# A long convolution beside a gated MLP: filter, convolution and most of the MLP in 64x64 TensorE tiles in place of 128x128 and 32x32

## The chip, the cores and the metric

One core of one Trainium2 chip. The metric is the device time of one execution in microseconds (us), the median of several runs; lower is better.

## What is computed

Two branches read the same layer-normed input. Branch A is a causal long convolution over 2048 positions in 512 channels, branch B a gated MLP with 1792 inner features.

```
xn = layernorm(A_q)                                   # 2048 x 512
kv = (sum over t of k shifted by t * shift_k[t]) * v   # four taps
y  = irfft(rfft(kv, 4096) * rfft(ssm_k, 4096))[:2048] + kv * ssm_D
s  = xn * y
h  = gelu(xn @ w_gate) * (xn @ w_up)                   # 512 -> 1792
out = A_q + s * silu(h @ w_down)                       # 1792 -> 512
```

All inputs and the output are bf16.

## The kernel before

**The convolution** is a transform of 4096 points in two stages. Stage 1 multiplies 128 partitions by a 128x256 matrix `F1` with full 128x128 matmuls (two per row tile, 512 columns each): for the filter from its transposed halves `HTr` and `HTD` (`half1`, `stage1_h`), for the key product from `V` (`stage1_k`). The results are evacuated, stored to the scratch tensors ZH and ZK in HBM and read back with other rows on the partitions, as `BH` and `BK`. Stage 2 is 32 small transforms of 32 points, each with its own twiddled matrix in `TF`; `tiles` (L1023 ff.) runs sixteen 32x32 matmuls side by side, one for each tile of the array, 512 columns each: `fwd` for BH and BK in eight groups. The filter's spectrum lands in `HS`, a copy with swapped partners is made by DMA (`HW`), VectorE multiplies both by the key's spectrum `KB`, and the inverse stage 2 (`inv` in `spectrum`) adds two rounds of sixteen tiles, with `MI`. `BO` is stored to ZI, read back as `BI`, and the output transform `y` (L1201) multiplies with `G1`, four full matmuls for two row tiles.

**The filter** comes with channels on the partitions. Half of it is transposed by TensorE (`h_transpose`, L878, pairs of bf16 read as one fp32 word), half by DMA (`HTD`).

**The MLP.** The 2048 rows are cut into four quarters of 512 (q = 0 to 3). `unit(q, m)` computes 128 inner features: four matmuls into a gate bank and four into an up bank of PSUM, a gelu on ScalarE (L1137), a product on VectorE (L1140). For q = 0 the first two units work in halves of 256 rows. `down(q)` computes each of four row tiles from fourteen matmuls (L1156); for q < 3 a tanh and a VectorE op make the gate from it, for q = 3 a silu, and the last row tile is cut into 384 and 128 columns.

**What sets the order.** All of this is a list of tasks. The string `SEQ` names them in the order in which they are issued, on all engines; a small model (`Sched.run`) only hands out buffer slots along the way. Each engine runs its own part strictly in this order, waiting on semaphores where data or a buffer is not ready; loads and stores are issued mostly from SP, some from ScalarE's queue. PSUM has eight banks, in four pairs. Nearly every TensorE, copy and DMA instruction is issued from one line (L618, L609, L612, L590), so the profile names them by their tiles: `psall<-xnT,Wu` is an up matmul, `psall<-Wd,HT` a down matmul, `psall<-V,F` stage 1 of the key, `psall<-BH,TF` and `psall<-BK,TF` forward stage 2 (L1028), `psall<-HS,MI` and `psall<-HW,MI` its inverse, `psall<-BI,G` the output transform, `psall<-ident,Hn` the filter's transposes.

Of the kernel before, what the change touches and what calls it, by code (L numbers as in the profile page):

```python
# [14 lines left out]
DM = 512  # L15
# [37 lines left out]
LOAD_NS = {("x0_", 262144): 1400.0, ("x0_", 131072): 450.0, 262144: 900.0, 524288: 1350.0, ("x", 524288): 2100.0, ("h", 524288): 1300.0, ("wg", 524288): 1550.0, ("wu", 524288): 1450.0, 917504: 2620.0, ("sk", 524288): 1500.0, 344064: 1250.0, 46080: 350.0, 3072: 100.0, 1024: 200.0}  # L53
# [5 lines left out]
N_HALF = 2  # L59

# [214 lines left out]
class Buf:  # L275


    def __init__(self, name, pool=None):
# [4 lines left out]
        self.readers = []  # L283
        self.left = 0
        self.last_end = 0.0


class Task:
    __slots__ = ("n", "opts", "r", "w", "emit", "deps", "lat", "nbytes", "start", "end", "eng", "outs", "heavy", "mode")


class Sched:


    SEM = 90.0
# [3 lines left out]
    DMA_BW = 370.0  # L299
    SHARE_BW = 300.0  # L300
    FIRST = {"loads": 1050.0, "SP": 30500.0}
    DRAIN = 121.0
    EARLY, TAKEN, SHARED, WAIT = (0.0, 1.0), 1400.0, 46000.0, 3300.0
    LANDS = (4350.0, 5590.0, 7100.0, 8420.0, 9350.0, 10200.0, 11500.0)

# [981 lines left out]
```

## Time and profile before

| | before |
|---|---|
| median of the timed runs (lowest, highest) | 194.69 us (194.65, 195.05) |
| span of the profiled execution | 193.3 us |
| TensorE matmuls, busy | 1377, 188.6 us |
| VectorE, ScalarE, GpSimd busy | 160.0, 125.4, 13.9 us |
| moved by DMA | 49.19 MB |

The profiled execution has no time of its own beside its span: the timed runs include 1.4 us more, around the span. "Busy" counts a matmul from its start to its modelled end, and these overlap. A row of a timeline gives the start, the length from the first start to the last end, the engine and line, out<-in, and how many instructions it merges; brackets hold idle time before it and who ended it. A row of a group ends with its count, busy time, the mean length of one in ns, and the idle time before its instructions.

### The profile page before, as it was taken

How to read it: one execution, taken by the hardware profiler on the slowest of the kernel's cores; microseconds unless marked ns; L12 is line 12 of the kernel's file. 1: busy time of each engine (PE TensorE's matmuls, PEld its weight loads, DVE VectorE, ACT ScalarE, POOL GpSimd, SP SyncE). 2: the span in 40 equal slices, each digit the busy share in tenths (PEclk: the TensorE clock that was granted, in tenths of full speed). 3: DMA queues.
4: the chain of work that ended last, by engine and by line, in shares of the span. 5: the costliest groups of instructions: out<-in, count | busy, mean ns of one | idle time of the engine just before them, and what ended most of it. 6: DMA issues, size and time to landing. Idle time of an engine off the chain costs nothing.

```text
span 193.3 us, 3502 instructions
## 1 busy us (share of the span) xinstructions
PE 188.6 (98%) x1377; PEld 85.6 (44%) x1377; DVE 160.0 (83%) x245; ACT 125.4 (65%) x170; POOL 13.9 (7%) x32
## 2 busy tenths in 40 slices
PE   7899999999999999999999999999999999999993
PEld 2685544444444444443434433433444334444452
DVE  6699789998999995877888789878897863588993
ACT  6787999969885987868548766856577431232121
POOL 5412420000000000020300000000000000000000
PEclk9999999999999999999999999999999999999999
DMA  5999999999999679999999991984805345939333
GB/s 175 311 307 349 377 400 347 157 249 372 375 374 354 196 264 259 390 323 305 218 285 230 338 320 59 288 276 147 264 10 195 106 140 153 389 112 353 132 139 136
DMA packets 45958, 49.19 MB, mean 254 GB/s; under 512 B 12787, under 2 KB 39671, under 8 KB 45942
## 3 DMA queue, kind: packets, MB, share of 16 engines
q1 hardware_dynamic: 37366, 42.67, 70.1%
q10 hardware_dynamic: 8576, 6.29, 10.3%
q8 instruction: 11, 0.18, 0.4%
q14 instruction: 5, 0.04, 0.1%
HBM read 27.39 MB, written 14.68 MB: 218 GB/s over the span
## 4 chain that ended last, share of the span: by engine, by line
PE 93%; DMA 4%; SPq 1%; DVE 1%; ACT 0%; issue 0%
PE psall L618 86%; PE psall L1028 5%; DMA Hn<-in_A_ssm_k_dram 4%; PE psall L854 1%; SPq L590 1%; PE psall L878 1%; DVE G L1175 0%; DVE G L1174 0%; ACT G L1172 0%
## 5 line engine op out<-in xcount | busy, mean ns | idle before, releaser
L618 PE MATMUL psall<-xnT,Wu 128*128 128x512 bf16 (+1 forms) x232 | 55.8, 372 | 0.0
L618 PE MATMUL psall<-xnT,Wg 128*128 128x512 bf16 (+1 forms) x232 | 55.3, 372 | 0.0
L618 PE MATMUL psall<-Wd,HT 128*128 128x512 bf16 (+2 forms) x238 | 52.0, 367 | 0.0
L1140 DVE TENSOR_TENSOR HT<-psall,GE 128x512 bf16<-128x512 f32 x54 | 36.7, 685 | 15.8 <-PE psall L618 15.4
L1137 ACT ACTIVATE GE<-psall 128x512 bf16<-128x512 f32 x54 | 31.7, 601 | 13.1 <-PE psall L618 12.9
L618 PEld LDWEIGHTS psall<-Wd,HT 128*128 128x128 bf16 x238 | 22.4, 98 | 25.9 <-issue 1.1
L618 PEld LDWEIGHTS psall<-xnT,Wg 128*128 128x128 bf16 x232 | 21.9, 98 | 25.4 <-issue 1.3
L618 PEld LDWEIGHTS psall<-xnT,Wu 128*128 128x128 bf16 x232 | 21.6, 98 | 25.9 <-issue 3.5
L609 ACT ACTIVATE X<-psall 128x1024 bf16<-128x1024 f32 (+1 forms) x18 | 15.1, 843 | 3.3 <-DMA ZH<-X 1.9
L609 ACT ACTIVATE HS<-psall 128x1024 bf16<-128x1024 f32 x14 | 13.7, 1022 | 4.4 <-PE psall L1028 4.4
L1164 ACT ACTIVATE G<-psall 128x512 bf16<-128x512 f32 x12 | 7.0, 598 | 12.9 <-PE psall L618 12.4
L1011 DVE TENSOR_TENSOR KAC<-KAC,KTM 128x2048 bf16<-128x2048 bf16 x12 | 14.6, 1217 | 0.1
L1009 DVE TENSOR_TENSOR KTM<-KK,SKB 128x2048 bf16<-128x2048 bf16 x12 | 14.6, 1217 | 0.0
L609 ACT ACTIVATE BO<-psall 128x1024 bf16<-128x1024 f32 x9 | 9.1, 1022 | 8.2 <-PE psall L1028 7.7
L609 ACT ACTIVATE KB<-psall 128x1024 bf16<-128x1024 f32 x11 | 11.0, 1021 | 3.6 <-PE psall L1028 3.6
L609 ACT ACTIVATE AST<-psall 128x1024 bf16<-128x1024 f32 x12 | 12.4, 1033 | 0.7 <-PE psall L618 0.5
L612 DVE CAST BO<-psall 128x1024 bf16<-128x1024 f32 x7 | 8.5, 1224 | 3.7 <-PE psall L1028 3.7
L821 DVE BATCH_NORM_STATS2 stats<-X 128x6 f32<-128x512 bf16 x16 | 10.3, 675 | 1.1 <-DMA X<-in_A_q_dram 1.1
L1172 ACT ACTIVATE G<-psall 128x512 bf16<-128x512 f32 (+2 forms) x5 | 2.6, 512 | 13.1 <-PE psall L618 13.1
L1091 DVE TENSOR_TENSOR HW<-KB,HW 128x1024 bf16<-128x1024 bf16 x16 | 10.9, 682 | 0.0
L1091 DVE TENSOR_TENSOR HS<-KB,HS 128x1024 bf16<-128x1024 bf16 x16 | 10.8, 682 | 0.0
L1166 DVE SCALAR_TENSOR_TENSOR G<-G,psall 128x512 bf16<-128x512 bf16 x12 | 7.8, 680 | 2.0 <-ACT G L1164 2.0
(83 smaller groups left out, 175.6 us busy)
## 6 DMA issues: line engine op xcount, KB each, us to landing
BH<-ZH SPq DMA_DIRECT2D x8, 512.0 KB, 6.1
HW<-HS SPq DMA_DIRECT2D x16, 256.0 KB, 3.2
BK<-ZK SPq DMA_DIRECT2D x8, 512.0 KB, 5.1
ZI<-BO ACTq DMA_DIRECT2D x16, 256.0 KB, 2.8
BI<-ZI SPq DMA_DIRECT2D x8, 512.0 KB, 4.2
ZK<-AST SPq DMA_DIRECT2D x6, 512.0 KB, 4.1
Hn<-in_A_ssm_k_dram SPq DMA_DIRECT2D x4, 512.0 KB, 8.4
KK<-in_A_k_dram SPq DMA_DIRECT2D x4, 512.0 KB, 8.6
```

The lines of the kernel that those rows point to most:

```text
L609: return h.activation(o, i, ACTF.Copy, scale=scale)
L612: return h.tensor_copy(o, i)
L618: return h.matmul(o, lhsT=l, rhs=r, start=st, stop=sp)
L821: t_stats[t] = op([("DVE", 670.0)], lambda e, h, t=t: h.bn_stats(stats[:, t, :], X[:, t, :]), r=[bX[q][t % 4]], w=[bst[t]], rr=[R_X[t]], w ...
L1009: op([("DVE", dur)], lambda e, h, j=j, m=m: h.tensor_tensor(KTM[:, m.slot, :, :], kk(j), sk(j), ALU.mult), r=need + [bSKB[j], a], w=[m], r ...
L1011: op([("DVE", dur)], lambda e, h, m=m: h.tensor_tensor(KAC[:, a.slot, :, :], KAC[:, a.slot, :, :], KTM[:, m.slot, :, :], ALU.add), r=[m], ...
L1028: trk.op("PE", lambda h: h.matmul(ps(s, i)[b, :], lhsT=wt(col)[a, :], rhs=data(col)[a, :], start=n < 16, stop=n >= len(todo) - 16, tile_po ...
L1091: return hd.tensor_tensor(o, flat(KB, kb[h]), o, ALU.mult)
L1137: op([("ACT", act(512))], lambda e, h: h.activation(GE[:, g.slot, :], bank(pg), ACTF.Gelu_apprx_tanh), r=[pg], w=[g], rr=lambda: R_bank(pg ...
L1140: op([("DVE", dve(512, 1))], lambda e, h: h.tensor_tensor(HT[:, q % 2, m, :], bank(pu), GE[:, g.slot, :], ALU.mult), r=[pu, g], w=[bHT[q][m]],
L1164: op([("ACT", act(n))], lambda e, h, g=g, pc=pc: h.activation(g, pc(), ACTF.Tanh, scale=0.5), r=[p], w=[bt], rr=lambda p=p: R_bank(p), ww= ...
L1166: op([("DVE", dve(512, 1))], lambda e, h, g=g, pc=pc: h.scalar_tensor_tensor(out=g, in0=g, scalar=1.0, in1=pc(), op0=ALU.add, op1=ALU.mult ...
```

## The change

Between the transposes of the filter and the last two row tiles, every matmul becomes a 64x64 tile of the array, four of them side by side making a round (`quads`). The rows of the sequence are dealt out so that the two halves of the partitions hold the even and the odd blocks of 16 rows (`rows`). The transform of 4096 points is split 64 by 32 on each half: stage 1 needs one round for what took two full matmuls, stage 2 has 64x64 matrices and takes two rounds where one round of sixteen tiles served. Tables (`TF`, `MI`, `TFA`) grow accordingly and are made by GpSimd where VectorE made them.

A 64x64 tile adds up 64 partitions only, and in the kernel the two row halves of the array always write different banks. So a unit and a pair of row tiles of `down` use a pair of banks in two phases: in the first, the lower half of the partitions adds to bank 0 and the upper to bank 1, in the second the other way round. The first matmul of the second phase waits for the end of the first (`own`, and `hand` in the list). The same holds for the output transform.

The filter's transposes are 64x64 bf16 matmuls with the identity. Four pairs of row tiles (`N_RAW`) are copied out raw, and get one silu of 1024 elements after the last gelu in place of a tanh each. `SEQ` is a new order, and the order of the loads changes with it. All ahead of the core is left out here: table making, addresses, names.

```diff
+        def quads(rounds, own=False, cols=None):
+            todo = [(n, *x) for n, x in enumerate(x for rnd in rounds for x in rnd)]
+            for n, pair, i, r, c, wt, data, rt, st, sp in todo:
+                w = R_ps[pair] if own and n == 0 else [R_ps[pair][i]]
+                trk.op("PE", lambda h: h.matmul(ps(pair, i)[HALF[c], cols(n) if cols else slice(0, 512)], lhsT=wt, rhs=data, start=st, stop=sp, tile_position=(64 * r, 64 * c)),
+                       r=rt, w=w, accum=not (own and n == 0), quiet=n < len(todo) - 1)
...
-                        trk.op("PE", lambda h, o=o, src=src: h.transpose(o, src, ident32[:]), r=[R_Hn[k], R_id32], w=R_bank(pp[hf]), accum=True)
+                quads([[(psl(p), r, r, b, src[HALF[r], 8 * hf + j, b, :], ident[HALF[r], HALF[r]], [R_Hn[k], R_id], True, True) for r in range(2) for b in range(2)] for j in range(8)], cols=lambda n: slice(64 * (n // 4), 64 * (n // 4) + 64))
...
+        def fwd1(pair, data, rd):
+            for b in range(2):
                 for c in range(2):
-                    trk.op("PE", lambda h, c=c: mm(h, bank(p)[:, 256 * c:256 * c + 256], F1[:, c, :], HTr[:, u, 256 * k:256 * k + 256], True, True), r=[R_F1, R_HTr[u][k]], w=R_bank(p), accum=True)
+                    o, n = slice(64 * c, 64 * c + 64), slice(64 * b, 64 * b + 64)
+                    trk.op("PE", lambda h: h.matmul(ps(pair, b)[o, :], lhsT=F1[n, o], rhs=data[n], start=True, stop=True, tile_position=(64 * b, 64 * c)),
+                           r=[R_F1, *rd], w=[R_ps[pair][b]], accum=True, quiet=b + c < 2)
...
-        def fwd(pp, T, R_T, buf, n):
-            return lambda e: tiles(pp, [(lambda c: TF[:, 4 * n + c, :], lambda c: T[:, buf.slot, c, :], [R_MF, R_T[buf.slot]])])
+        def fwd(p, T, R_T, buf, n, h):
+            return lambda e: quads([[(psl(p), r, r, c, TF[HALF[r], 4 * n + 2 * h + c, :], T[HALF[r], buf.slot, 2 * h + c, :], [R_MF[n // 4], R_T[buf.slot]], True, True) for r in range(2) for c in range(2)]])
...
-            def inv(e):
-                tiles(pi, [(lambda c, m=m: MI[:, m, n, 32 * c:32 * c + 32], lambda c, T=T, b=b: T[b.slot][:, c, :], [R_MI[m], *R_b])
             for h in range(2):
+                def inv(e, h=h):
+                    quads([[(psl(pi[h]), r, r, c, MI[HALF[r], m, 2 * n + h, 64 * c:64 * c + 64], T[b.slot][HALF[r], 2 * h + c, :], [R_MI[m], *R_b], m == 0, m == 1) for r in range(2) for c in range(2)]
...
-            tg = S.add([("PE", pe(4))], half(pg, Wg, "g"), r=[bW["g"][ci]] + bxnT[q], w=[pg], lat=200.0)
-            tu = S.add([("PE", pe(4))], half(pu, Wu, "u"), r=[bW["u"][ci]] + bxnT[q], w=[pu], lat=200.0, after=[tg])
+            def phase(ph):
+                def f(e):
+                    quads([[(psl(p), (r + ph) % 2, r, c, (Wg, Wu)[(r + ph) % 2][HALF[r], kd, 128 * m + 64 * c:128 * m + 64 * c + 64], xnT[HALF[r], q % 2, 0:4, kd, :],
+                             [R_Wc["gu"[(r + ph) % 2], ci], *R_xnT[q % 2]], ph == 0 and kd == 0, ph == 1 and kd == KD - 1) for r in range(2) for c in range(2)] for kd in range(KD)], own=ph == 1)
+            hand = None
+            for ph in range(2):
+                hand = S.add([("PE", 4 * T_ROUND)], phase(ph), r=[bW["g"][ci], bW["u"][ci]] + bxnT[q], w=[p], lat=200.0, mode=1, hand=hand)
...
+            for i, (ph, m0, m1) in enumerate(((0, 0, 4), (0, 4, 9), (1, 0, 4), (1, 4, 9), (1, 9, 14), (0, 9, 14))):
+                own = i in (2, 5)
+                hand = S.add([("PE", (m1 - m0) * T_ROUND)], part(ph, m0, m1, i == 0, i == 5, own), r=bHT[q][m0:m1] + bWd[m0 // 7:(m1 + 6) // 7], w=[p], lat=200.0, mode=1, hand=hand if own else None)
...
-                        trk.op("PE", lambda h, i=i, c=c: mm(h, ps(s, i), G1[:, c, :], BI[:, bi.slot, 2 * i + c, :], c == 0, c == 1),
+                    quads([[(psl(p), (r + ph) % 2, r, c, G1[HALF[r], 0:64], BI[HALF[r], bi.slot, 2 * ((r + ph) % 2) + c, :], [R_G1, R_BI[bi.slot]], ph == 0, ph == 1) for r in range(2) for c in range(2)]], own=ph == 1)
...
+            if j < N_RAW:
+                op([("ACT", act(1024, True))], lambda e, h, g=g: h.activation(g, g, ACTF.Silu), r=[bG[j]], w=[bGX[j]], rr=R_G[ts], ww=R_G[ts], after=gelu_tasks)
```

Three places of TensorE's order show what it moves. First the start: the beginning of TensorE's list before, from the second filter block (h1) on.

```order
L878 MATMUL psall<-ident_63,Hn 128x128 x8
L618 MATMUL psall<-xnT,Wg 128x256 x4
L618 MATMUL psall<-HTr,F_58 128x256 x2
L854 MATMUL psall<-ident,XN 128x128 x4
L618 MATMUL psall<-xnT,Wu 128x256 x4
```

And of the change, from the x transposes behind the first filter block (h0), with what each waits for; d_wg1 and d_wu1 are the landings of the second group of weights:

```order
L858 MATMUL psall<-ident,XN 128x128 [waits s_DVE]
L858 MATMUL psall<-ident,XN 128x128 x3
L620 MATMUL psall<-xnT,Wu 128x256 [waits d_wu0,s_DVE]
L620 MATMUL psall<-xnT,Wu 128x256 x3
L620 MATMUL psall<-xnT,Wg 128x256 [waits d_wg0]
L620 MATMUL psall<-xnT,Wg 128x256 x3
...
L933 MATMUL psall<-HTr,F_55 64x512 [waits s_ACT]
L933 MATMUL psall<-HTr,F_55 64x512 x3
L878 MATMUL psall<-xnT,Wg 64x512 [waits d_wg1,s_DVE]
L878 MATMUL psall<-xnT,Wg 64x512
L878 MATMUL psall<-xnT,Wu 64x512 [waits d_wu1,s_ACT]
```

The h1 block has moved behind the first units in 64x64 tiles, and between the first weights and those units only half units and one round of stage 1 are left. Second, the hand-over on TensorE where units and stage 1 of the key mix: behind a unit's first phase comes other work, then its second phase, which waits for TensorE's own semaphore.

```order
L878 MATMUL psall<-xnT,Wu 64x512 x2
L933 MATMUL psall<-V,F_55 64x512 [waits s_ACT]
L933 MATMUL psall<-V,F_55 64x512
L933 MATMUL psall<-V,F_55 64x512 [waits s_DVE]
L933 MATMUL psall<-V,F_55 64x512
L933 MATMUL psall<-HTD,F_55 64x512 [waits s_ACT]
L933 MATMUL psall<-HTD,F_55 64x512 x3
L878 MATMUL psall<-xnT,Wu 64x512 [waits s_PE]
```

Two rounds of stage 1 lie between the phases here. There are 76 such hand-overs; between the phases lie no round in 5 of them, one in 10, two or more in 61. Third, the first inverse transforms, before:

```order
L618 MATMUL psall<-Wd,HT 128x512 x14
L1028 MATMUL psall<-HS_56,MI 32x512 x16
L1028 MATMUL psall<-HW_96,MI 32x512 x16
L618 MATMUL psall<-xnT,Wg 128x512 x8
L618 MATMUL psall<-xnT,Wu 128x512 x4
```

and of the change, among forward transforms of the key and the phases of units:

```order
L878 MATMUL psall<-BK,TF 64x512 x8
L878 MATMUL psall<-Wd,HT 64x512 x20
L878 MATMUL psall<-xnT,Wg 64x512 x2
L878 MATMUL psall<-xnT,Wu 64x512 x2
...
L878 MATMUL psall<-HS_93,MI 64x512 x4
L878 MATMUL psall<-HW_95,MI 64x512 x4
L878 MATMUL psall<-xnT,Wu 64x512 x2
```

All shapes are now the same here; the list has 128x128 matmuls left in the warm-up, the transposes of x with the half units (at two places), and the last two row tiles. In all TensorE has 3205 matmuls in place of 1377.

More of the change, by code (lines that the diff above doesn't have):

```diff
@@ L59 @@
 N_HALF = 2
+N_RAW = 4
 class Res:
@@ L288 @@
 class Task:
-    __slots__ = ("n", "opts", "r", "w", "emit", "deps", "lat", "nbytes", "start", "end", "eng", "outs", "heavy", "mode")
+    __slots__ = ("n", "opts", "r", "w", "emit", "deps", "lat", "nbytes", "start", "end", "eng", "outs", "heavy", "mode", "hold", "hand")
 class Sched:
@@ L317, in add @@
         t.start = t.end = t.eng = None
-        t.mode = mode
+        t.mode, t.hold, t.hand = mode, list(hold), hand
         deps = {}
@@ L333, in add @@
             b.writers.append(t)
-        for b in set(t.r + t.w):
+        for b in set(t.r + t.w + t.hold):
             b.left += 1
@@ L356, in run @@
                 base = max(base, d.end if eng == d.eng == "PE" else d.end + d.lat + (self.SEM if not d.nbytes or eng != "PE" else 400.0 if d.eng == "loads" else self.HEDGE))
-            for b in t.w:
+            if t.hand is not None:
+                base = max(base, t.hand.end + self.HAND)
+            for b in t.w + t.hold:
                 if b.pool is not None and b.slot is None:
@@ L376, in run @@
                 t.end = pipe + self.DMA_LAT / 2 + (self.WAIT if en < self.SHARED else 0.0)
-            for b in set(t.r + t.w):
+            for b in set(t.r + t.w + t.hold):
                 b.left -= 1
@@ L474, in build_kernel @@
         place["at"] = kk_at + 2048
[L475 to L476 removed]
+        HS = [new(f"HS{j}", [128, 4, DM], BF16) for j in range(3)]
+        HW = [new("HW0", [128, 4, DM], BF16), *[at(f"HW{j}", [128, 4, DM], BF16, ast_at + 4096 * (j - 1)) for j in (1, 2)]]
         KB = new("KB", [128, 4, 2, DM], BF16)
@@ L604, in emit @@
                 trk.op(e, lambda h: fn(e, h), r=R, w=W)
-            return S.add(engs, emit, r=r, w=w, lat=lat, after=after)
+            return S.add(engs, emit, r=r, w=w, lat=lat, after=after, hold=hold)
         def copy(e, h, o, i, scale=1.0):
@@ L890, in build_kernel @@
+        for k in range(2):
+            for hf in range(2):
+                h_transpose(k, hf)
         h_perm, h_dtr = [], []
@@ L936, in stage1_h @@
             if x == "H" and u >= 4:
-                for k in range(2):
-                    half1(u, k, a)
+                aH[u] = a
+                if u % 2:
+                    for k in range(2):
+                        half1(u - 1, k)
             else:
@@ L1020, in z_rows @@
             return bass.AP(Z, g * 128 * DM, [[DM, 128], [128 * DM, n], [1, DM]])
-        def tiles(pp, terms):
-            todo = [(wt, data, rt, row, col) for wt, data, rt in terms for row in range(4) for col in range(4)]
-            for n, (wt, data, rt, row, col) in enumerate(todo):
-                a, b = slice(32 * row, 32 * row + 32), slice(32 * col, 32 * col + 32)
-                s, i = psl(pp[row // 2]), row % 2
-                trk.op("PE", lambda h: h.matmul(ps(s, i)[b, :], lhsT=wt(col)[a, :], rhs=data(col)[a, :], start=n < 16, stop=n >= len(todo) - 16, tile_position=(32 * row, 32 * col)),
-                       r=rt, w=[R_ps[s][i]], accum=True, quiet=n < len(todo) - 1)
@@ L1181, in build_kernel @@
+        def down(q):
+            down_pair(q, 0)
+            if q < NQ - 1:
+                down_pair(q, 2)
+                return
+            for jt in (2, 3):
+                down_tile(q, jt)
         for q in range(NQ):
```

386 lines of the change are left out of this document (199 added, 187 removed), and 45 rows, old and new, of the table SEQ.

## The prediction

> **What bounds the kernel now.** I read the page's busy lines first, then the chain of waits in order of time, then who waited for whom on TensorE, then TensorE's groups by shape. The page and the chain:
>
> ```profile
> PE 188.6 (98%) x1377; PEld 85.6 (44%) x1377; DVE 160.0 (83%) x245; ACT 125.4 (65%) x170; POOL 13.9 (7%) x32
> ...
> PEclk9999999999999999999999999999999999999999
> ...
> PE 93%; DMA 4%; SPq 1%; DVE 1%; ACT 0%; issue 0%
> ```
>
> ```profile
> 2.12 7.16 DMA Hn<-in_A_ssm_k_dram
> ...
> 30.27 51.16 PE psall L618 x238
> 81.42 0.36 PE psall L1028 x16
> ...
> 189.55 0.02 issue
> ```
>
> The waits of TensorE behind its first real matmul at 5.64 us are two short ones:
>
> ```profile
> PE psall L878 <- DMA Hn<-in_A_ssm_k_dram: 0.5, 1, 0.5
> PE psall L618 <- ACT HTr L609: 0.2, 1, 0.2
> ```
>
> So from 9.3 to 189.6 us TensorE runs without a gap at full clock, and what its work costs is what the kernel costs: a nanosecond taken out of TensorE's stream is a nanosecond of time, as long as nobody makes it wait instead. The span is 193.3 us; the timed runs have a median of 194.69, so 1.4 us lie around the span, and I carry that over. The stream, by shape (count | busy us, mean ns):
>
> ```profile
> L618 PE MATMUL psall<-xnT,Wu 128*128 128x512 bf16 x216 | 53.6, 380 | 0.0
> ...
> L618 PE MATMUL psall<-Wd,HT 128*128 128x512 bf16 x210 | 49.0, 379 | 0.0
> L618 PE MATMUL psall<-V,F 128*128 128x512 bf16 x32 | 9.2, 379 | 0.0
> L618 PE MATMUL psall<-BI,G 128*128 128x512 bf16 x32 | 7.6, 379 | 0.0
> ...
> L618 PE MATMUL psall<-HTD,F 128*128 128x512 bf16 x16 | 4.6, 379 | 0.0
> L1028 PE MATMUL psall<-BK,TF 32*32 32x512 bf16 x128 | 3.5, 385 | 0.0
> L1028 PE MATMUL psall<-HS,MI 32*32 32x512 bf16 x128 | 3.5, 385 | 0.0
> L1028 PE MATMUL psall<-BH,TF 32*32 32x512 bf16 x128 | 3.5, 385 | 0.0
> L1028 PE MATMUL psall<-HW,MI 32*32 32x512 bf16 x128 | 3.4, 374 | 0.0
> ...
> L618 PE MATMUL psall<-HTr,F 128*128 128x256 bf16 x16 | 2.9, 274 | 0.2 <-ACT HTr L609 0.2
> ...
> L618 PE MATMUL psall<-HTr,F 128*128 128x512 bf16 x8 | 2.4, 379 | 0.0
> ```
>
> The 379 ns is one matmul from start to end; they overlap. The pace, and the price of changing the tile shape, come from the timeline of TensorE around one inverse transform:
>
> ```profile
> 97.45 3.20 PE L618 MATMUL psall<-Wd,HT 128*128 128x512 bf16 x14
> 100.58 0.43 PE L1028 MATMUL psall<-HS,MI 32*32 32x512 bf16 x16
> 100.81 0.42 PE L1028 MATMUL psall<-HW,MI 32*32 32x512 bf16 x16
> 101.16 1.90 PE L618 MATMUL psall<-xnT,Wg 128*128 128x512 bf16 x8
> ```
>
> Fourteen matmuls take 3.20 us, the last of them 0.379: (3.20 - 0.379) / 13 = 0.217, and over longer runs 0.216 us each. A "round" of sixteen 32x32 tiles with 512 columns takes as long as one full matmul: HS to HW is 0.23 us. From 97.45 to 101.16 are 3.71 us for 14 matmuls and 2 rounds, 16 x 0.216 = 3.46: going into 32x32 tiles and out again costs **0.25 us**. The four L1028 rows hold 512 / 16 = 32 rounds in 24 such visits (8 forward H, 8 forward K, 8 inverse with two rounds).
>
> **The change, part by part**, on TensorE's stream. A round is now four 64x64 matmuls with 512 columns, priced at 0.216: the same array, fully covered, as a full matmul. Both tiled and full rows above show that pace, but no row shows a 64x64 round; the bounds are 0.216 below (two forms so different keep it, and neither is faster) and 0.234 above (worked out under the rivals).
>
> 1. Stage 1 and the output transform do half the work each. Before: 32 + 16 + 8 + 32 full matmuls and 16 of half width, (88 + 8) x 0.216 = 20.7 us. Now 32 rounds of stage 1 and 16 of the output, 48 x 0.216 = 10.4. **-10.3 us.**
> 2. Stage 2 does twice the work: 32 rounds become 64 (16 forward H, 16 forward K, 32 inverse). **+6.9 us.**
> 3. The switches go: 24 x 0.25 = 6.0. By the order, the new stream has three stretches of 128x128 left (the transposes of x with half units, twice, and the last two row tiles), so three trips, one of which lies in the idle start. Two on the path, 0.5. **-5.5 us.**
> 4. The units and the down projections keep their work: 432 full matmuls of the units become 432 rounds, 196 of the 210 full ones of the down projections become 196 rounds. 0 us.
> 5. The filter's transposes:
>
> ```profile
> 5.64 1.71 PE L878 MATMUL psall<-ident,Hn 128*128 128x128 f32 x8
> 7.18 0.39 PE L854 MATMUL psall<-ident,XN 128*128 128x128 bf16 x4
> ...
> 9.32 1.16 PE L878 MATMUL psall<-ident,Hn 128*128 128x128 f32 x8 [0.46 <-DMA Hn<-in_A_ssm_k_dram]
> ```
>
> Before 1.71 + 1.16 = 2.9 us. Now 32 rounds of 64 columns, not shown in any row: between 64/512 x 0.216 = 0.027 each and the pace of a 128-column transpose, (0.39 - 0.22) / 3 = 0.057, so 0.9 to 1.8. I take 1.3, the middle. **-1.6 us.**
>
> 6. New is that TensorE waits for itself. A unit's first phase fills the two banks from one half of the partitions each, the second phase adds the other half, and its first matmul waits for the end of the first phase. What such a wait costs bare:
>
> ```profile
> 101.34 1.02 ACT L609 ACTIVATE BO<-psall 128x1024 bf16<-128x1024 f32 x1 [2.15 <-PE psall L1028]
> ```
>
> The reader of the round that began at 100.81 (above) starts 101.34 - (100.81 + 0.42) = 0.11 after its end. A bare hand-over then costs 0.379 + 0.11 - 0.216 = 0.27 us beyond the pace; one round in between leaves 0.05, two hide it. The order has 76 of them: 5 bare, 10 with one round between, 61 with two or more. 5 x 0.27 + 10 x 0.05 = **+1.9 us**. Behind a waiting matmul stands all of TensorE, and behind that the evacuations of ScalarE and VectorE, which have slack (65% and 83% busy). The other bound is 76 x 0.27 = 20 us, if filler did not hide the wait; the gapless stream between 24 visits whose results others wait for speaks against it.
>
> 7. The start. Before, the second filter block (h1) is transposed from 9.32 on and fills the time until weights land. Now x tiles 2 and 3 and the first weights are loaded ahead of h1, and the first 64x64 unit needs both weights of the second group (2.5 MB into the loads). The old landings give the rate:
>
> ```profile
> 3.08 0.70 SPq L590 DMA_DIRECT2D Wu<-in_B_w_up_dram  x1
> ...
> 5.10 0.66 SPq L590 DMA_DIRECT2D KK<-in_A_k_dram  x1
> ```
>
> ```profile
> Wu<-in_B_w_up_dram SPq DMA_DIRECT2D x1, 256.0 KB, 7.9
> KK<-in_A_k_dram SPq DMA_DIRECT2D x1, 336.0 KB, 11.0
> ```
>
> Wu's first part ended 2.0 MB at 3.08 + 7.9 = 11.0, the halo 3.35 MB at 16.1; h1 ended 1.5 MB at 9.3 (chain). 2.5 MB land at 11.0 + 0.5 x 5.1 / 1.35 = 12.9, by the earlier rate at 12.7; I take 12.8. Ahead of it TensorE has only h0's transposes (0.65), four x transposes (0.9), four half units (1.7) and one round (0.2), 3.5 us from 5.6 on: 12.8 - 5.6 - 3.5 = 3.7 idle, against 0.7 before. **+3.0 us**; between +1.5 (the loads 1.5 us faster) and +4.5.
>
> 8. The end. VectorE's list behind the last pair of row tiles of the third quarter is some 5 us long and TensorE's rest 6.1 us; the last result waits a little more for VectorE. **+0.3 us** (0 to 0.6). The two table products and the sum move from VectorE to GpSimd, the tanh of four pairs of row tiles becomes a copy with a later silu; both lie beside TensorE's work, nothing in the profile waits for them for the next 50 us, and I cost them at nothing.
>
> Sum: -10.3 + 6.9 - 5.5 - 1.6 + 1.9 + 3.0 + 0.3 = **-5.3 us**: a span of 188.0, and 194.69 - 5.3 = **189.4 us**.
>
> [...] First the row, of the same inverse transform:
>
> ```profile
> 100.63 0.14 PEld L1028 LDWEIGHTS psall<-HW,MI 32*32 32x32 bf16 x16
> ```
>
> All sixteen loads of the second round start at 100.63, while the sixteen matmuls of the first run in every row group until 100.81, and the second round starts on time: the loads were covered. [...]
>
> **Rivals.**
>
> *A: the tiled pace is 226, not 216 (slower than before).* The two rounds at 100.58 and 100.81 stand 0.226 apart to the nanosecond rounding, 10 ns more than full matmuls. If that belongs to every tiled round, all 740 rounds (432 + 196 + 48 + 64) pay it: +7.4 us, **196.8 us**. It decides from 5.3 / 740 = 7 ns per round. Against it: the first matmul behind a switch back to 128x128 shows the same surplus (3.71 - 3.46 holds it), so it looks like a price of entry.
>
> *B: others make TensorE wait.* VectorE and the DMA engines are nearly full where stage 1 of the key runs:
>
> ```profile
> 36.00:72.00 36.00, 36.00 (x169) 16.29 (x168) 35.03 (x38) 29.77 (x40) 0.00 (x0) 1.00 0.96 299
> ```
>
> VectorE is busy 35.0 of 36 us, DMA 0.96. TensorE gets 24 rounds (5.2 us) less to do there. If VectorE's list holds it, up to all of that comes back as waits; half of it gives **192.0 us**. The other place is the return of the inverse transform: from its last round to the first output round the order has 45 rounds, 9.7 us; the way there is a copy (1.02), a store and a load,
>
> ```profile
> ZI<-BO ACTq DMA_DIRECT2D x16, 256.0 KB, 2.8
> BI<-ZI SPq DMA_DIRECT2D x8, 512.0 KB, 4.2
> ```
>
> 8.0 us and some tenths of issue; a late load costs what it is late. For B: these margins. Against: units of other quarters fill TensorE, as they do now.
>
> *C: the instructions don't come fast enough.* 3205 matmuls instead of 1377. The densest long stretch:
>
> ```profile
> 150.20:157.35 7.15, 7.15 (x122) 2.78 (x122) 5.07 (x7) 3.51 (x5) 0.00 (x0) 1.00 0.23 81
> ```
>
> 122 matmuls in 7.15 us, 59 ns each with its load; a 64x64 round needs 216 / 4 = 54. If 59 were the limit, 0.234 per round, +13.5 us, **203 us**. Sixteen start (0.43 - 0.385) / 15 = 3 ns apart within a round, which speaks against it, though a queue could have held them.
>
> [...]
>
> *E: the start is not held and hand-overs hide*: terms 6 and 7 nearly vanish, **186 us**.
>
> **Chances.** Forecast 0.62, A 0.08, B 0.20, C 0.03, D 0.02, E 0.05. The range 186.6 to 194.0 takes in the bounds of terms 5 to 8 and most of B. Faster by over 0.2% (what a measurement here can tell from no change): forecast, E and nearly all of B, 0.85; within 0.2%: 0.02; slower: A, C, D, 0.13.
>
> **What the profile after would show.** Right: rounds 0.216 apart in long runs; an idle stretch of some 3 us before 13 us and hardly any later; output transform half as long; waits of TensorE on itself of 0.3 us at five places. Wrong: rounds of 0.226 or more (A, C, D), or gaps behind VectorE or DMA between 36 and 100 us or ahead of the first output round (B).

## The result, and the profile after

The changed kernel takes **329.52 us** (median of 4 runs, 328.23 to 331.39) beside 194.87 us for the kernel before on the same chip (4 runs, 194.65 to 195.06): a ratio of **1.691**, 95% interval 1.684 to 1.697. The forecast was 189.4 us. The profiled execution of the changed kernel spans 326.4 us. (Some runs of a kernel are over 1.5% longer than its fastest, in e5_natural 209.79 and 211.53 us at a granted clock of 0.965 and 0.967 beside 206.13 to 206.58 at 0.975: medians below are over all runs, but differences between kernels with 64x64 tiles leave such runs out.) First its page, with TensorE, clock, DMA and GB/s in 40 slices of 8.2 us, and the chain that ended last:

```profile
PE 200.4 (61%) x3204; PEld 104.9 (32%) x3205; DVE 166.4 (51%) x245; ACT 130.3 (40%) x166; POOL 25.8 (8%) x37
...
PE   5093667369500000391889967999999999994000
...
PEclk9999595959975555587699996999999999999555
DMA  2765345414211191885757938996894467411111
GB/s 74 202 217 152 114 162 150 121 54 138 79 52 52 52 67 52 192 188 139 171 186 268 220 98 273 332 261 200 302 356 157 174 219 244 151 53 51 51 48 43
...
SPq 36%; PE 33%; DMA 17%; ACT 2%; issue 2%; DVE 1%; DVEq 0%
```

TensorE, 93% of the chain before, is a third of it now. The first place is held by SPq, SyncE standing in the issue of a DMA. TensorE's row has a hole of five slices, a ragged start and an empty end. In the hole (but for one slice) and at the end the DMA row stands at 1 and the last row near 50 GB/s. Windows of the changed kernel (from:to and length, busy us of TensorE, of its weight loads, VectorE, ScalarE, GpSimd; granted clock, busy share of the 16 DMA engines, GB/s):

```profile
67.00:110.00 43.00, 18.06 (x266) 8.00 (x266) 9.04 (x10) 11.79 (x13) 0.00 (x0) 0.74 0.20 74
110.00:135.00 25.00, 0.00 (x0) 0.00 (x0) 0.28 (x2) 0.00 (x0) 0.00 (x0) 0.50 0.85 76
200.00:285.00 85.00, 85.00 (x1554) 45.59 (x1550) 66.81 (x94) 56.57 (x73) 1.28 (x2) 0.99 0.72 240
285.00:326.00 41.00, 11.89 (x149) 6.43 (x139) 11.22 (x20) 2.46 (x5) 0.00 (x0) 0.70 0.13 50
```

The last row says what it is: 50 GB/s at a busy share of 0.13, and 0.13 x 16 is **2 DMA engines**. Most of that stretch has only stores of `out` left. By the trace no load or store that `rows` addresses is issued between 181 and 279 us, and in the row above TensorE has no gap.

The chain of the changed kernel in order of time (start, length, what) shows what fills the hole:

```profile
66.27 9.94 SPq L592
76.20 0.04 issue
76.25 11.07 SPq L592
87.36 11.22 SPq L592
98.58 0.04 issue
98.62 10.05 SPq L592
108.67 0.04 issue
108.72 23.83 SPq L909
132.55 0.05 issue
132.60 4.63 DMA HTD<-HP
137.28 0.04 issue
137.32 0.70 DVE HT L1165
```

By the trace the first four are loads of a key or value tile, 512 KB each: SyncE gets one off every 10 to 11 us, about 50 GB/s. Behind them stands the filter's transposing DMA (L909). VectorE's timeline, then who waited for whom on VectorE and on TensorE, carry it on:

```profile
102.36 1.23 DVE L1024 TENSOR_TENSOR KAC<-KK,SKB 128x2048 bf16<-128x2048 bf16 x1 [16.23 <-DMA KK<-in_A_k_dram]
134.72 0.28 DVE L917 TENSOR_TENSOR HTD<-HTD,Drow 1x256 bf16<-1x256 bf16 x1 [31.14 <-DMA HTD<-HP]
```

```profile
DVE HTD L917 <- DMA HTD<-HP: 31.1, 1, 31.1
```

```profile
PE psall L878 <- DVE HT L1165: 49.7, 2, 47.1
```

VectorE waits 16 us for a key tile and, one instruction later, 31 us for the transposed filter; the product that frees a bank stands behind both in VectorE's list, and TensorE waits 47 us for that product. Nothing of this is in the tiles. It is in a line that the prediction passed by, the addresses of x, k, v and out in HBM:

```diff
+        def rows(A, t0, n, c0=0, c1=DM):
+            return bass.AP(A.tensor, A[0].offset + t0 * DM + c0, [[16 * DM, 2], [32 * DM, 64], [DM, n], [1, c1 - c0]])
```

The kernel before read block p of 16 rows into partition p, one dimension of 128. Even blocks to the lower and odd blocks to the upper partitions makes this two dimensions, the outer of size 2.

### The profile page after: what moved, and what is told of

It reads as the page before. It is cut to its first block, busy times and chain, and to the rows that moved or that the text cites. A ratio compares the mean times of both kernels' runs of the same rounds, so it can differ in the third digit from the quotient of the medians.

```text
span 326.4 us, 7135 instructions
## 1 busy us (share of the span) xinstructions
PE 200.4 (61%) x3204; PEld 104.9 (32%) x3205; DVE 166.4 (51%) x245; ACT 130.3 (40%) x166; POOL 25.8 (8%) x37
## 4 chain that ended last, share of the span: by engine, by line
SPq 36%; PE 33%; DMA 17%; ACT 2%; issue 2%; DVE 1%; DVEq 0%
PE psall L878 30%; SPq L592 28%; SPq L909 7%; DMA BH<-ZH 5%; DMA Hn<-in_A_ssm_k_dram 4%; DMA BI<-ZI 3%; PE psall L620 2%; DMA G<-F 2%; DMA Wd<-in_B_w_down_dram 2%; DMA HTD<-HP 1%; PE psall L933 1%; ACT ASX L611 1%; ACT G L611 1%; SPq L1053 1%; ACT TFA L730 0%
## 5 line engine op out<-in xcount | busy, mean ns | idle before, releaser
L878 PE MATMUL psall<-xnT,Wu 64*64 64x512 bf16 x864 | 112.2, 402 | 50.7 <-DVE HT L1165 49.7
L878 PE MATMUL psall<-xnT,Wg 64*64 64x512 bf16 x864 | 112.9, 402 | 6.6 <-DMA Wg<-in_B_w_gate_dram 6.6
L878 PEld LDWEIGHTS psall<-xnT,Wu 64*64 64x64 bf16 x864 | 48.4, 113 | 80.6 <-DVE HT L1165 51.1
L878 PEld LDWEIGHTS psall<-xnT,Wg 64*64 64x64 bf16 x864 | 48.8, 113 | 28.9 <-issue 10.7
L878 PE MATMUL psall<-Wd,HT 64*64 64x512 bf16 x784 | 50.9, 386 | 3.5 <-issue 1.8
L878 PEld LDWEIGHTS psall<-Wd,HT 64*64 64x64 bf16 x784 | 24.5, 109 | 23.9 <-issue 3.2
L611 ACT ACTIVATE AST<-psall 128x1024 bf16<-128x1024 f32 x11 | 11.2, 1024 | 51.0 <-DVE HTD L917 46.4
L1024 DVE TENSOR_TENSOR KAC<-KK,SKB 128x2048 bf16<-128x2048 bf16 x4 | 4.8, 1212 | 20.1 <-DMA KK<-in_A_k_dram 20.1
L611 ACT ACTIVATE X<-psall 128x1024 bf16<-128x1024 f32 (+1 forms) x13 | 11.0, 856 | 8.9 <-PE psall L933 4.7
L839 DVE TENSOR_SCALAR XN<-X,mv 128x512 bf16<-128x512 bf16 x16 | 12.5, 821 | 1.4 <-POOL mv L836 1.4
L933 PE MATMUL psall<-V,F 64*64 64x512 bf16 x64 | 8.6, 432 | 7.4 <-DVE HT L1165 7.4
```

What stands on the lines that cost most here:

```text
L611: return h.activation(o, i, ACTF.Copy, scale=scale)
L839: op([("DVE", 420.0)], lambda e, hd, t=t: hd.tensor_scalar(XN[:, t, :], X[:, t, :], mv[:, t, 0:1], mv[:, t, 3:4], ALU.subtract, ALU.mult), ...
L878: trk.op("PE", lambda h: h.matmul(ps(pair, i)[HALF[c], cols(n) if cols else slice(0, 512)], lhsT=wt, rhs=data, start=st, stop=sp, tile_pos ...
L933: trk.op("PE", lambda h: h.matmul(ps(pair, b)[o, :], lhsT=F1[n, o], rhs=data[n], start=True, stop=True, tile_position=(64 * b, 64 * c)), r ...
```

## The experiments

### Is it the loads and stores, and is it their leading dimension?

**e1_two_dmas** writes each of these DMAs as two of 64 partitions:

```diff
-            return bass.AP(A.tensor, A[0].offset + t0 * DM + c0, [[16 * DM, 2], [32 * DM, 64], [DM, n], [1, c1 - c0]])
+            return [bass.AP(A.tensor, A[0].offset + (t0 + 16 * r) * DM + c0, [[32 * DM, 64], [DM, n], [1, c1 - c0]]) for r in range(2)]
```

> The change with each load of x, k and v and each store of out issued as two DMAs of 64 partitions instead of one whose DRAM pattern has a leading dimension of 2; nothing else differs. Theory 1 (the leading dimension of 2 confines such a DMA to 2 of the 16 DMA engines, so that 512 KB take 10.6 us instead of 1.5 to 2; all else of the prediction stands): 189.4 us, 186.6 to 194.0. Theory 2 (the even and odd blocks of rows, 32 KB apart in DRAM, are slow to read whatever the pattern): over 250. Theory 3 (the loads are only a part of it, the 64x64 tiles are slower than priced): 194 to 250, with TensorE's rounds at more than 0.22 us in the profile.

**lead4** and **lead16** keep one DMA and only enlarge the outer dimension:

```diff
-[[16 * DM, 2], [32 * DM, 64], [DM, n], [1, c1 - c0]]
+[[16 * DM, 4], [64 * DM, 32], [DM, n], [1, c1 - c0]]      # lead4
+[[16 * DM, 16], [256 * DM, 8], [DM, n], [1, c1 - c0]]     # lead16
```

> The change with a leading dimension of 4 instead of 2 in these patterns, still one DMA each. The two axes of rows are then dealt otherwise to the partitions (block 4b+a of 16 rows on partition 32a+b, instead of block 2b+a on 64a+b), so the convolution joins other blocks than it should; the work of every engine is the same. Theory 1 (as many DMA engines as the leading dimension): 512 KB in about 5.3 us, the time between e1_two_dmas and the change, near the middle: 225 to 265 us. Theory 2 (addresses): as the change, 320 to 340, since the strides in DRAM only get longer.

> The same with a leading dimension of 16 (block 16b+a on partition 8a+b; the convolution joins other blocks than it should, the work of every engine is the same). Theory 1: all 16 DMA engines, so the time of e1_two_dmas or, as half as many DMAs are issued, up to 2 us less: 186 to 192 us. Theory 2 (addresses): over 250 us.

**before_lead2** does this part of the change alone, on the kernel before:

```diff
-        x_dr = A_q[0].rearrange("(p t) d -> p t d", t=NT)     # k, v and out likewise
+        def rows(A, t0, n, c0=0, c1=DM):
+            return bass.AP(A.tensor, A[0].offset + t0 * DM + c0, [[16 * DM, 2], [32 * DM, 64], [DM, n], [1, c1 - c0]])
```

> The kernel before with only the change's patterns for x, k, v and out (leading dimension of 2, even blocks of 16 rows on the lower 64 partitions); tiles, order and transforms are those of before, and the convolution joins other blocks than it should. Theory 1: the loads and stores alone cost what the change lost, 8 MB at some 49 GB/s instead of 250: 194.7 + 135 = 330 us, 300 to 350. Theory 3 (64x64 tiles are a part of it): nearer 195 than 330.

Measured: e1_two_dmas 219.12 us (6 runs; 1.118 of before, 1.115 to 1.122), lead4 256.11 (one run), lead16 216.20 (4 runs; 1.102, 1.099 to 1.106), before_lead2 330.62 (one run). With 128x128 and 32x32 tiles and not one other line changed, the pattern makes the kernel before as slow as the change: theory 1 holds, and theory 2 falls with lead4 and lead16, whose strides are longer. The ends of before_lead2 and of lead4, in windows:

```profile
295.00:328.00 33.00, 1.55 (x19) 1.11 (x17) 1.49 (x5) 0.77 (x2) 0.00 (x0) 0.56 0.13 49
```

```profile
234.00:254.00 20.00, 9.33 (x105) 5.05 (x98) 8.91 (x16) 2.45 (x5) 0.00 (x0) 0.82 0.25 92
```

That is 2 engines and 49 GB/s with an outer dimension of 2, 4 engines (0.25 x 16) and 92 GB/s with 4.

But the half of theory 1 that said "all else of the prediction stands" is refuted: 219 and 216 are not 189. Some 27 us are something else, and theory 3's "TensorE's rounds" it isn't (below).

### Two suspects in e1_two_dmas, both missed

In e1_two_dmas TensorE idled 4.5 us behind VectorE while GpSimd made the tables, and ScalarE waited 3.5 us for slow stores of the filter's first stage. **e2_tables_dve** puts the table work back on VectorE (in `SEQ` a `b` picks the second engine), **e3_late_kv** delays two key and two value loads, **e4_both** does both:

```diff
-... 104b 13b 416 ... 490b 14b 15b 16b 147 148 17b 18b 492 ...
+... 104b 13 416 ... 490b 14 15 16 147 148 17 18 492 ...            # e2, e4
-... 41 42 45 46 487 ... 60 47 48 153 62 442 443 63 64 448 ...
+... 41 42 487 ... 60 153 62 442 443 63 64 45 46 47 48 448 ...      # e3, e4
```

> e1_two_dmas with the six table products and sums (128x1024) on VectorE, where they were before, instead of on GpSimd. In e1_two_dmas VectorE's four normalisations of x stretch from 0.41 to 1.37 us each and two products of the key from 1.21 to 2.5 and 3.4, from 25.7 to 39.2 us, while GpSimd makes the tables from 26.7 to 38.2; TensorE waits 4.5 us for the normalised x there and then runs at half clock. Theory 4 (GpSimd's table work blocks VectorE): these durations go back to 0.41 and 1.21, the 4.5 us of waits nearly vanish and 2 us of half clock with them: 219 - 6.5 = 212.6 us, 210 to 215. Theory 5 (the order of the loads alone delays it): 217 to 222, with the stretched durations still there or the waits for other things.

> e1_two_dmas with the loads of the last two key tiles and value tiles (2 MB) issued behind the two transposing DMAs of the filter instead of ahead of them. Theory 5 (the stores of the filter's first stage, 256 KB each, share the DMA engines with 3 MB of key and value loads that are not needed yet: they land after 11 to 27 us instead of 7, ScalarE's staging tiles come free late, then SyncE's queue, and with them the waits of 2.4 us near 50 and 5.6 us near 80, and their half clock): 219 - 8 to 12 = 207 to 211. Theory 4 (GpSimd only): 217 to 221, the stores' late landing hidden by other work.

> Both edits of e2_tables_dve and e3_late_kv on top of e1_two_dmas. If both theories hold and add up: 201 to 206 us, with TensorE idle only in the start (some 3.5 us) and the forecast's pace behind it; what then is left above 189.4 is the late start and clock. If only one holds: 208 to 213.

Measured: 216.58 and 218.34 us (one run each) and 219.97 (4 runs; 1.127, 1.119 to 1.135). Neither edit gives what it was expected to, and both together give nothing. In e2 the suspect did go, the four normalisations took 1.53 us in place of 5.48, without the gain; in e3 it did not, the four stores still took 11.7 to 18.0 us to land. I took this to mean that something ahead of both was wrong, in the transfers.

### Half of the partitions, half of the speed

Ten microseconds at the start of four kernels, before, e1_two_dmas, lead16 and (below) e5_natural; the last two numbers are the busy share of the DMA engines and GB/s:

```profile
10.00:20.00 10.00, 9.98 (x74) 6.41 (x73) 9.93 (x22) 8.05 (x15) 1.85 (x3) 1.00 1.07 330
```

```profile
10.00:20.00 10.00, 7.35 (x117) 4.72 (x116) 5.87 (x17) 4.78 (x9) 1.24 (x1) 1.00 1.05 239
```

```profile
10.00:20.00 10.00, 9.25 (x154) 6.38 (x152) 7.68 (x19) 6.41 (x10) 1.81 (x1) 0.90 1.05 261
```

```profile
10.00:20.00 10.00, 9.61 (x192) 6.58 (x196) 7.34 (x18) 6.57 (x11) 2.56 (x4) 1.00 1.06 328
```

All 16 engines are busy in each, but they move 239 or 261 GB/s in place of 330. By the trace's packets, those of 4096 bytes took 316 ns (median, 10 to 12 us) in e1_two_dmas and 264 in lead16, against 159 to 166 in the kernel before. **before_two** splits the DMAs of the kernel before into two of 64 partitions; **e5_natural** gives the changed kernel the old patterns, and **e6_natural_dve** adds the edit of e2:

```diff
-            args = X[:, 4 * q:4 * q + 4, :], x_dr[:, 4 * q:4 * q + 4, :], R_X[4 * q:4 * q + 4], bX[q]
+            args = two(X[:, 4 * q:4 * q + 4, :]), two(x_dr[:, 4 * q:4 * q + 4, :]), R_X[4 * q:4 * q + 4], bX[q]   # before_two; two(ap) = [ap[0:64], ap[64:128]]
...
-[[16 * DM, 2], [32 * DM, 64], [DM, n], [1, c1 - c0]]
+[[16 * DM, 128], [DM, n], [1, c1 - c0]]                   # e5_natural, e6_natural_dve
```

> The kernel before with each of its loads of x, k and v and its stores of out issued as two DMAs of 64 partitions; nothing else differs and the rows lie as before. [...] If only the even and odd blocks were slow: 194 to 196.

> The change with the rows dealt to the partitions as before (block p of 16 rows on partition p, one DMA of 128 partitions); the convolution joins other blocks than it should, the work of every engine is the same. In e1_two_dmas and lead16 the packets of 4096 bytes took 260 to 316 ns between 10 and 32 us, in the kernel before 159 to 166. [...] Theory 4 (GpSimd's tables are enough to hold it): 196 to 206, with the normalisations still at 1.4 us and a wait behind them. Theory 5 (the order of the loads, hand-overs of the 64x64 tiles): over 206.

> e5_natural with the six table products and sums on VectorE instead of GpSimd. Theory 4: 2 to 7 us under e5_natural. [...]

Measured: before_two 209.47 us (one run), e5_natural **206.58** (5 runs; 1.060, 1.057 to 1.064), e6_natural_dve 209.79 (one run). before_two shows it without any of the change: the same bytes, rows and order, two DMAs for one, and 15 us more, above the 197 to 206 that I had expected from packets of some 316 ns. It also issues these DMAs twice, but its packets of 4096 bytes took 325 ns (median, 10 to 12 us), twice those of the kernel before, and lead16, with as many DMAs as the change, is slow too (264 ns). Why packets to 64 partitions take longer, and why lead16, whose DMAs have 128 partitions, lies between, no run shows.

In e5_natural these packets are back at 165 ns and the first loads at 328 GB/s, but the time lies above the 189.4 to 196 that I had expected if the loads were the whole of it: with plain loads the change stands at 206.6, 12 us above the kernel before and 17 above the forecast. The one run of e6 again shows no gain.

### The last 17 us

In e5_natural TensorE waits between 23 and 34 us and at 73 us:

```profile
PE psall L858 <- DVE XN L839: 5.4, 4, 3.2
PE psall L878 <- DMA Wd<-in_B_w_down_dram: 4.9, 1, 4.9
```

**e7_wd_early** loads the second half of the down weights right behind the first; **e8_no_tables** leaves out nearly all table work:

```diff
-... 455 43 493 ... 140 141 44 465 ...
+... 455 43 44 493 ... 140 141 465 ...                              # e7
...
-            trk.op(e, lambda h: h.tensor_tensor(TM[i][:], a, b, ALU.mult), ...
+            trk.op(e, lambda h: h.tensor_tensor(TM[i][:, 0:1, :], a[:, 0:1, :], b[:, 0:1, :], ALU.mult), ...   # e8
-            trk.op(e, lambda h: h.tensor_tensor(TF[:, 16 * hf:16 * hf + 16, :], TM[0][:], TM[1][:], ALU.add), ...
+            trk.op(e, lambda h: h.memset(TF[:, 16 * hf:16 * hf + 16, :], 0.125), ...                           # e8, on VectorE
```

> e5_natural with the load of the second half of the down projection's weights issued right behind that of the first half, instead of behind three transposing DMAs and eight stores on SyncE's queue. In e5_natural it is issued at 71.6, lands at 77.6, and TensorE waits 4.9 us for it and then runs about 4 us at half clock. Theory 7 (this wait, in SyncE's queue, is a cost of its own): no wait there, 206.6 - 4.9 - 2 = 199.7 us, 198 to 202. Theory 8 (what held SyncE, the late first stage of the filter, holds the next consumer too): the wait moves to another place, 203 to 207.

> e5_natural with the table work of GpSimd left out: three products of 128x64 instead of four of 128x1024 stay, and the two sums are memsets on VectorE, so the twiddle table holds a constant (the transforms' results are not the reference's; every other instruction stays). In e5_natural TensorE idles 6.9 us between 23.5 and 33.6, behind VectorE's four normalisations that take 8.2 us in place of 1.6 while GpSimd makes the tables, and then runs at half clock for some 4 us. Theory 4 (GpSimd's table work blocks VectorE, and so TensorE): normalisations at 0.41, 206.6 - 6.9 - 2 = 197.7 if nothing else holds it there, 196 to 202. Rival (ScalarE stands 4.2 us in the issue of its third and fourth store of the filter's first stage, 22.4 to 26.6, and holds the same matmuls): 202 to 206.

Measured: e7 203.49 us (1.043, 1.034 to 1.053), e8 208.31 (1.069, 1.062 to 1.076), 4 runs each. e7's trace no longer has the wait, but it gains 3.4 us, half of what was expected; e8 gains nothing, though what its edit does on VectorE is plain. (Its trace has four products of 128x64, not three.) VectorE's four normalisations of x and GpSimd in e5_natural (two queries, the first instruction alone, then all four; and GpSimd's own), then VectorE in e8_no_tables:

```profile
25.23 1.89 DVE L839 TENSOR_SCALAR XN<-X,mv 128x512 bf16<-128x512 bf16 x1
...
25.23 8.19 DVE L839 TENSOR_SCALAR XN<-X,mv 128x512 bf16<-128x512 bf16 x4
```

```profile
24.64 2.34 POOL L718 TENSOR_TENSOR TF<-TM,TM 128x1024 bf16<-128x1024 f32 x1
27.06 3.81 POOL L715 TENSOR_TENSOR TM<-TAB 128x1024 f32<-128x1024 f32 x2
30.94 2.34 POOL L718 TENSOR_TENSOR TF<-TM,TM 128x1024 bf16<-128x1024 f32 x1
```

```profile
22.23 1.38 DVE L842 TENSOR_SCALAR XN<-X,mv 128x512 bf16<-128x512 bf16 x4
```

The four take 8.19 us in place of 1.38. The first ends at 27.12, GpSimd's sum at 26.98; the last ends at 33.42, GpSimd's last sum at 33.28: both end 0.14 us behind the end of a sum on GpSimd. How GpSimd holds VectorE there no run shows. That leaving the tables out gains nothing in e8 is, I take it, because the next wait is due at the same time. ScalarE in e8_no_tables:

```profile
33.48 1.02 ACT L614 ACTIVATE X<-psall 128x1024 bf16<-128x1024 f32 x1 [1.05 <-DMA ZH<-X]
38.80 1.02 ACT L614 ACTIVATE X<-psall 128x1024 bf16<-128x1024 f32 x1 [4.30 <-DMA ZH<-X]
```

It wants to copy out a round of the filter's first stage and has no staging tile: four stores of 256 KB, issued within 2.3 us of each other, land after 7 to 17 us, with key and value loads beside them (in e10 below, without these loads, after 7.5 to 8.7 us). **e9_stores_on_sp** puts these four on SyncE's queue ahead of those loads, **e10_late_kv** puts the loads behind the filter's transposing DMAs, **e11_sp_no_tables** is e9 with e8's edit. All three have e7's:

```diff
-S.add([("ACT", 350.0) if x == "H" else ("SP", ISSUE)], st, ...
+S.add([("ACT", 350.0), ("SP", ISSUE)] if x == "H" else [("SP", ISSUE)], st, ...   # e9, e11
-... 109 ... 117 ... 110 118 ... 28 41 42 45 46 ...
+... 28 109b 117b 110b 118b 41 42 45 46 ...                         # e9, e11
-... 28 41 42 45 46 ... 47 48 ... 63 64 448 ...
+... 28 ... 63 64 41 42 45 46 47 48 448 ...                         # e10
```

> e7_wd_early with the first four stores of the filter's first stage issued by SyncE, ahead of the loads of three key and three value tiles, instead of by ScalarE beside them. In e5_natural and e8_no_tables these four (256 KB each, issued within 2 us) land after 9 to 16 us, packet by packet with 4096-byte loads, hold ScalarE 2 to 4 us in their issue and keep all staging tiles until 33 to 39 us, so that ScalarE stands 4 to 5 us before its next evacuation. Theory 5 (stores and loads collide there): ScalarE's issue stall gone, staging tiles free by 35, 203.5 - 4 = 199.5 us, 197 to 201.5. Theory 4 (GpSimd's tables are what is left): 202 to 205.

> e7_wd_early with the last three key tiles and last three value tiles loaded behind the two transposing DMAs of the filter, so that nothing but weights shares the DMA engines with those four stores. Theory 5: the stores land within 8 us of their issue, the staging tiles are free by 31 us, the waits of ScalarE there go: 197 to 201 us; but the key's first stage may then wait for its loads near 50 to 60 us, which gives it back: 201 to 205, with the wait named by a key or value tile.

> e9_stores_on_sp with the table work of GpSimd left out as in e8_no_tables (the twiddle table holds a constant). Theories 4 and 5 together (each alone is hidden behind the other): 191 to 196 us, near the forecast's 189.4. If something else holds the stretch of 20 to 70 us: over 198.

Measured, 4 runs each: e9 206.90 us (1.054, 1.048 to 1.060), e10 210.92 (1.085, 1.078 to 1.091), e11 **200.29** (1.025, 1.017 to 1.033). By itself e9 is no gain over e7 (2.4 us slower); with the tables gone as well it is 5.0 us better. But e11 misses its 191 to 196 too: by its expectation something else holds the stretch of 20 to 70 us. e10 gives back more than it takes, at the place that its expectation named as a danger: VectorE waits 8.3 us for a key tile, and TensorE's wait is put down to the product that stands behind the key's work in VectorE's list:

```profile
PE psall L881 <- DVE HT L1168: 7.7, 3, 7.3
```

Three more. **e12_stores_lead2** is e5_natural with only the stores of `out` on the change's pattern (which then puts rows of out in other places than the reference does), **e13_tables_early** is e9, all its work included, with a product and a sum of the table earlier on GpSimd, **e14_clean_list** is e11 with what is left of the table work earlier:

```diff
-[[16 * DM, 128], [DM, n], ...
+([[16 * DM, 2], [32 * DM, 64]] if A is out else [[16 * DM, 128]]) + [[DM, n], ...   # e12
-... 104b 13b 416 ... 490b 14b 15b 16b ...
+... 104b 13b 14b 15b 416 ... 490b 16b ...                          # e13
-... 104b 13b 416 ... 477 409 ... 490b 14b 15 16b 147 148 17b 18 ...
+... 104b 416 ... 477 13b 14b 15 16b 17b 18 409 ... 490b 147 148 ...   # e14
```

> e5_natural (plain 128-partition loads) with only the stores of out on the change's pattern with its leading dimension of 2, which tells the share of the stores from that of the loads. Theory 1: 2 MB at 49 GB/s are 43 us of transfer, the last 1.4 MB or so behind TensorE's last work as in the change, where 28 us lie behind the last result against some 4: 206.6 + 24 = 231 us, 224 to 236; the loads of x, k and v then carry the other 90 to 100 us of the change's loss.

> e9_stores_on_sp, complete, with the second product and the first sum of the table moved ahead of the shift weights' copies on GpSimd, right behind the first product (about 12 to 18 us), where VectorE mostly reads PSUM. Theory 4: the normalisations of x then meet less of GpSimd's work, half of the 6.7 us between e9 (206.9) and e11 (200.3) comes back: 202 to 205 us. If the normalisations, which wait for GpSimd's reciprocal root behind those tables, come later instead: 206 to 209.

> e11_sp_no_tables with what is left of the table work (three products of 128x64 and two memsets) moved ahead, where GpSimd and VectorE are idle, so that VectorE's list between 24 and 31 us holds no memset and no wait for GpSimd. Theory 9 (what is left above the forecast is VectorE's in-order list there, which lets a product that frees TensorE's banks stand behind work on the key): waits of TensorE between 29 and 37 us shrink, 197 to 199 us. Otherwise 200 to 201, and the rest stays open.

Measured: e12 237.95 us (one run), e13 203.85 (4 runs; 1.044, 1.036 to 1.053), e14 199.81 (4 runs; 1.024, 1.018 to 1.031). The stores alone cost 237.95 - 206.58 = 31 us, somewhat more than the 24 expected, most of it in a bare tail of 28 us on two engines:

```profile
208.00:236.00 28.00, 0.00 (x0) 0.00 (x0) 0.05 (x1) 0.00 (x0) 0.00 (x0) 0.56 0.13 48
```

The loads cost the other 329.5 - 238.0 = 92. e13 gets 2.1 of e11's 5.0 us and keeps all the work, near the half that was expected. e14 is e11 within the intervals, and TensorE's waits between 29 and 37 us add up to 2.7 us in both: theory 9, VectorE's list, falls. No kernel of the study with 64x64 tiles reached the kernel before.

## Why the prediction was wrong, point by point

**The step that failed** is one that the prediction did not write down except inside term 7, "the old landings give the rate": x, k, v and out were taken to move as before, in their new addresses too, so their transfer was put at nothing without a reason. Term 8 and the forecast's last stores rest on the same. This cost 123 us (329.5 - 206.6). The price, though not the share of the engines, could have been had from the profile before:

```profile
20.00:30.00 10.00, 10.00 (x60) 5.03 (x59) 8.07 (x12) 9.37 (x15) 3.41 (x4) 1.00 1.07 392
```

392 GB/s on 16 busy engines are 24.5 GB/s for one, so two move 49, and 8.4 MB of x, k, v and out at 49 GB/s are 171 us, close to the whole forecast. That an outer dimension of 2 gets two engines (0.13 x 16 at the changed kernel's end) stands in no row of that profile. What was missing was to look at each DMA's pattern, not only at its place in the order.

*Terms 1 to 4, TensorE's work,* held. The chain of e11_sp_no_tables has one piece without a wait:

```profile
96.05 93.45 PE psall L881 x1724
```

1724 / 4 = 431 rounds in 93.45 us are 0.2168 each, beside 0.216 in the prediction. Rivals A (0.226), C (0.234) and D (the weight loads in the open) fall; 64x64 weight loads are covered too, as the 32x32 rows had said: in e11_sp_no_tables from 70 to 189.5 us, 66.62 us of them lie beside matmuls that are busy for all of the 119.50 us.

*Term 5, the filter's transposes,* was too small. In e5_natural:

```profile
6.92 1.96 PE L878 MATMUL psall<-ident,Hn 64*64 64x64 bf16 x64 [0.50 <-DMA Hn<-in_A_ssm_k_dram]
...
12.88 0.38 PE L878 MATMUL psall<-xnT,Wg 64*64 64x512 bf16 x2
...
16.54 1.86 PE L878 MATMUL psall<-ident,Hn 64*64 64x64 bf16 x64
```

One block takes 1.96 us and the other 1.86, together 3.8, where the prediction had 1.3 and an upper bound of 1.8: the term is +0.9, not -1.6. A 64x64 transpose takes 1.96 / 64 = 31 ns, and four make a round of 0.12 us, not 0.04.

*Term 6, the hand-overs,* cost at most what was priced: 431 rounds at 0.2168 beside 0.216 leave some tenths of a microsecond for all of them in that piece, and in no run do the waits of TensorE's matmuls name TensorE.

*Term 7, the start.* The idle time before the first 64x64 unit came out smaller with plain loads: 1.2 us up to 12.88 (waits of 0.50, 0.41 and 0.32 us), not 3.7. That this unit still starts where the forecast had it (12.8) is luck: the first real matmul comes at 6.92 in place of 5.64, and the first block's transposes take 1.3 us more than was forecast. In the change itself the first block of the filter is transposed at 16.86 us.

*Term 8.* The end costs what it did (e5_natural's last matmul ends 3.0 us before the span's end, in the kernel before 3.0). But "both lie beside TensorE's work ... I cost them at nothing" was wrong for the tables. They are also not "two table products and the sum" but four products and two sums, 12.3 us on GpSimd in e5_natural where VectorE took 3.6 before. They are worth 5.0 us (e9 against e11), once the stores of the filter don't hide them; what they would cost there on VectorE no run shows.

*Rival B* was right in kind, that others make TensorE wait, and its price was not: at most 5.2 us, at VectorE's list beside the key. The waits came from DMA, through VectorE's list, and the longest is 47 us.

*What is left.* e14_clean_list, with plain loads, early weights, stores on SyncE and hardly a table, is 10.4 us above the forecast, and the run of its trace, 200.7 us, 11.3. In that trace TensorE's idle time between 23 and 70 us adds up to 5.6 us, most of it waits for ScalarE and VectorE of 0.2 to 1.3 us each, and behind 70 us to 0.9; half clock makes 1.7 (last section) and the second block of transposes 1.2; the first 64x64 unit starts at 12.29, 0.5 ahead of the forecast. That is 8.9; over 2 us are not assigned, and the waits for ScalarE were not taken apart by a run. Why e9 alone gains nothing is open too.

## What to carry to other kernels

When a change deals the same bytes out in a new way, read every DMA's pattern before any engine's work. Here the rate went with its outermost dimension (49 GB/s with a 2, 92 with a 4) and with the partitions that it covers (from 10 to 20 us, 263 GB/s in before_two in place of 330), and a 2 as outermost dimension outweighed every term of the sum more than tenfold. When a suspect's removal gains nothing, look for a second wait that is due at the same moment and take both away together before calling either harmless.

## What the runs showed of the hardware

With an outermost dimension of 2 or 4 on the HBM side, 49 and 92 GB/s were moved at the ends of before_lead2 and lead4; with 16, in lead16, the loads from 10 to 20 us, weights among them, moved 261, beside 330 in the kernel before. The kernel before with two DMAs of 64 partitions for each of 128 (before_two) took 209.5 us (one run) against 194.8. VectorE's bf16 normalisation took 0.35 us (1.38 / 4) in e8_no_tables, and 2.0 us (8.19 / 4) in e5_natural, where GpSimd multiplied and added fp32 tables beside it.

Behind two short waits TensorE's granted clock was halved. Two neighbouring windows of e14_clean_list:

```profile
32.54:35.95 3.41, 1.81 (x28) 0.65 (x29) 2.88 (x4) 3.41 (x4) 0.00 (x0) 1.00 0.98 366
35.95:39.36 3.41, 3.35 (x36) 1.27 (x32) 3.38 (x4) 3.41 (x4) 0.00 (x0) 0.50 1.03 419
```

In the first it was busy for 1.81 of 3.41 us, with two waits of 0.3 and 1.3 us. For the whole second it had a granted clock of 0.50, though it was busy for 3.35 us of it, 36 matmuls where the pace gives 63. What halved the clock no run shows by itself; what it cost here is, by an estimate from the second row, half of 3.41, up to 1.7 us beside the waits.
